# Low-rank coefficients of a batch from two matrix products instead of five

## The chip, the cores and the metric

The kernel runs on one core of one Trainium2 chip. The metric is the device time of one execution in microseconds (us), the median of three runs. The core has five engines that work side by side, each through its own instruction queue in order: TensorE (PE in the profile; its weight loads are listed apart as PEld), VectorE (DVE), ScalarE (ACT), GpSimd (POOL) and SyncE (SP), which here only issues DMA transfers.

## The reference

The input `x` has 8 batches of 3136 rows and 256 channels. The first stage is the real part of a Fourier transform over rows and channels; the second adds a low-rank mixing over the rows and a two-layer network over the channels.

```python
X = np.fft.fft(x, axis=1)
X = np.fft.fft(X, axis=2)
x = X.real
h = x.transpose(0, 2, 1) @ U @ V        # U: 3136 x 32, V: 32 x 3136
u = x + h.transpose(0, 2, 1)
out = u + np.maximum(u @ w_ch1, 0.0) @ w_ch2   # 256 -> 1024 -> 256
```

The large products run in bf16 with fp32 sums.

## The kernel before

The output is made in 49 chunks of 512 rows that run across the batch borders. The main loop has 8 slots a chunk (`first_product(c, j)`, j = 0 to 7): each slot makes one 128x512 piece of the hidden layer (two products, line 691) and ScalarE applies the relu (line 693); every second slot also makes a row tile of the chunk before (`second_product`, eight products of 128x256, line 707), which VectorE adds to the transposed input and writes to `o` (lines 713 to 716). In slot 3 `front(c + 1)` builds the input `u` of the next chunk: one product adds the low-rank part (`low_product`, line 665), VectorE adds the transform `S` or `T` (line 681).

Between these, the work of the next batch is laid into the slots by `spread`: a list of steps is spaced evenly between a first and a last slot. `fold(b)` (VectorE, lines 386 to 399, with the loads of the next batch, issued by GpSimd's queue) ends before `transform(b)`, which for batches 2 to 7 has 17 steps: eight calls of `seq`, four pairs of `even_ch` and `odd_ch`, and `lowrank`. Batches 0 and 1 are done in another way: batch 0 ahead of the loop, batch 1 with `first_channel` and `chan` in its list. A scheduler then orders the instructions of each engine; the part ahead of the loop has the order in which it is written.

`seq(b, par, typ, pn)` multiplies the folded input by tables of sines (`typ` 0) and cosines (`typ` 1) along the rows; `par` says whether even or odd rows. The tables carry 32 further columns, `NQ:QW`, that hold the matching transform of U. So each `seq` with `pn` = 1 also gives a 128x32 piece, and there are four pieces a batch: two types by two parities. Before, line 459 writes each into its own 32 columns of `TAB`, in bf16. The folded sine half has nothing in partition 0 and row 0 of the sine matrix `MSN` is zero.

The channel that the halves leave over goes its own way (`narrow`): for batches 0 and 1 in `first_channel`, for batches 2 to 7 together in `column_steps`, which loads a single channel of six batches (`cf`, `cr`). `narrow` also gives the 32 coefficients of that channel: two parities, added at line 537 to a row of `low` (batches 0 and 1) or to a 6x32 tile; `finish` then spreads the six rows over `low` with one masked product each (line 573).

`lowrank(b)` brings these together in one PSUM tile: `low` times a matrix of ones, and the four pieces of `TAB` times the channel matrices `MSN` and `MC`. Line 636 copies the first 32 rows to `TA`, which `low_product` reads for all chunks of the batch.

Of the kernel before, what the change touches and what calls it, by code (L numbers as in the profile page):

```python
# [16 lines left out]
P = 128  # L17
# [3 lines left out]
NQ = 393  # L21
# [6 lines left out]
def kernel(  # L28
# [261 lines left out]
    def kp(i):  # L290
        return KP if i == NI - 1 else PQ
# [124 lines left out]
        for par in range(2):  # L416
            yield lambda par=par: half(b, par, slice(0, 258 if b < B0 else 256))

    TAB = cpool.tile([P, 7 * R], BF16, name="tab")
    NM = NQ // 2  # L420
    HW = QW - NM

    def halves(d, g, par, typ):

        pt = psum.tile([P, 2, 256], FP32, tag="dft", name="pth", bufs=3)
        for m, tiles in enumerate(((3, 7), (1, 5))):
            for n, i in enumerate(tiles):
                nc.tensor.matmul(pt[:, m, :HW], g[:kp(i), i, P * typ:P * (typ + 1)],  # L428
                                 tabs[typ][:kp(i), i, par, NM:], start=(n == 0), stop=(n == 1))
        ev = d["ev"] = wp.tile([P, QW], FP32, tag="ev", name="ev", bufs=4)  # L430
        nc.scalar.copy(ev[:, NM:], pt[:, 1, :HW])
        back = ev[:, NM - 1:(0 if par else None):-1]
        he, ho = pt[:, 0, 1 + par:NM + 1], ev[:, NM + 1 + par:NQ]
        nc.vector.tensor_tensor(back, *((he, ho) if typ == 1 else (ho, he)), op=AL.subtract)
        nc.vector.tensor_tensor(ev[:, NM:], pt[:, 0, :HW], ev[:, NM:], op=AL.add)

    def seq(b, par, typ, pn):

        if b not in ST:
            d = ST[b] = {}  # L440
            d["A"] = wp.tile([P, HALF + 1], BF16, tag="A", name="A", bufs=1)
            d["B"] = wp.tile([P, HALF + 1], BF16, tag="B", name="B", bufs=1)
            d["S"] = wp.tile([P, HALF + 1], BF16, tag="S", name="S", bufs=2)
            d["T"] = wp.tile([P, HALF + 1], BF16, tag="T", name="T", bufs=2)
        d = ST[b]
        g = G[b % 2][par]
        if pn == 0 and (b >= B0 or b == 1 and typ == 1):
            halves(d, g, par, typ)
            return
        pt = psum.tile([P, QW], FP32, tag="dft", name="pt", bufs=3)  # L450
        for n, i in enumerate(ktiles(pn)):
            nc.tensor.matmul(pt[:], g[:kp(i), i, P * typ:P * (typ + 1)], tabs[typ][:kp(i), i, par, :],  # L452
                             start=(n == 0), stop=(n == NI // 2 - 1))
        if pn == 0:
            ev = d["ev"] = wp.tile([P, QW], FP32, tag="ev", name="ev", bufs=4)
            nc.scalar.copy(ev[:], pt[:])
            return
        ev = d["ev"]
        nc.vector.tensor_tensor(TAB[:, (2 * typ + par) * R:(2 * typ + par + 1) * R],  # L459
                                pt[:, NQ:QW], ev[:, NQ:QW], op=AL.add)  # L460
        dst = d["A"] if typ == 1 else d["B"]
        if par == 0:
            up, c0 = dst[:, HALF // 2::-2], 0
        else:
            up, c0 = dst[:, HALF // 2 - 1:0:-2], 1
        nc.vector.tensor_tensor(up, pt[:, c0:NQ], ev[:, c0:NQ], op=AL.add)

        def down():
            dn = dst[:, HALF // 2 + 2 - par:HALF + 1 - par:2]
            nc.vector.tensor_tensor(dn, *((ev[:, 1:NQ], pt[:, 1:NQ]) if typ == 1 else  # L470
                                          (pt[:, 1:NQ], ev[:, 1:NQ])), op=AL.subtract)
        if b == 0 and typ == 1:
            return down
        down()
# [4 lines left out]
    cr = cpool.tile([KP, 2, NI, NB], FP32, name="cr")  # L479
    GC = [cpool.tile([KP, NI * NB + R], BF16, name=f"gc{par}", tag=f"gc{par}") for par in range(2)]  # L480
    rows = cpool.tile([NB, S], BF16, name="rows")
    low = cpool.tile([P, (B + 3) * R], BF16, name="low")
    unit = cpool.tile([P, NB], FP32, name="unit")

    def column_zeros():
        nc.gpsimd.memset(cf[:], 0.0)
        nc.gpsimd.memset(cr[:], 0.0)
        for par in range(2):
            nc.gpsimd.memset(GC[par][:, NI * NB:], 0.0)

    def column_flips():
        nc.vector.tensor_copy(unit[:], fl[:, 1, :NB])

    def column_loads():

# [18 lines left out]
    def narrow(nb, stationary, dst, tc_, total, tag=("dft", 3), late=None):  # L514

        t = {}

        def products():
            pt = t["pt"] = psum.tile([P, QW], FP32, tag=tag[0], name="ptc", bufs=tag[1])
            for n in range(NI // 2):  # L520
                for g in range(4):
                    pn, par = divmod(g, 2)
                    i = ktiles(pn)[n]
                    nc.tensor.matmul(pt[g * R:(g + 1) * R], stationary(par, i),
                                     tabs[1][:kp(i), i, par, :],
                                     start=(n == 0), stop=(n == NI // 2 - 1))
            t["ev"] = wp.tile([P, QW], FP32, tag="ev", name="evc", bufs=4)
            nc.scalar.copy(t["ev"][2 * R:], t["pt"][:2 * R])
        yield products

        def sums(par):
            e, o = (t[k][(2 + par) * R:(2 + par) * R + nb] for k in ("ev", "pt"))
            up = dst[:, HALF // 2 - par:(0 if par else None):-2]
            dn = dst[:, HALF // 2 + 2 - par:HALF + 1 - par:2]
            nc.vector.tensor_tensor(tc_[:, par], o[:, NQ:QW], e[:, NQ:QW], op=AL.add)
            if par:
                nc.vector.tensor_tensor(total, tc_[:, 0], tc_[:, 1], op=AL.add)
            nc.vector.tensor_tensor(up, o[:, par:NQ], e[:, par:NQ], op=AL.add)
            down = lambda: nc.vector.tensor_tensor(dn, e[:, 1:NQ], o[:, 1:NQ], op=AL.subtract)
            if late is None:  # L540
                down()
            else:
                late.append(down)
        for par in range(2):
            yield lambda par=par: sums(par)

    def column_steps():
# [3 lines left out]
        def fold_c():  # L551
# [11 lines left out]
            for par in range(2):  # L563
# [1 line left out]
                                        op=AL.add if par == 0 else AL.subtract)  # L565
        yield fold_c
        yield from narrow(NB, lambda par, i: GC[par][:kp(i), i * NB:i * NB + R], rows, tc_,
                          tc_[:, 0])

        def finish():  # L570
            nc.scalar.copy(rows[:, HALF + 1:S], rows[:, HALF - 1:0:-1])
            for b in range(NB):
                nc.vector.tensor_single_scalar(low[:NB, (b + B0) * R:(b + B0 + 1) * R], tc_[:, 0],
                                               unit[:NB, b:b + 1], op=AL.mult)
        yield finish

    def first_channel(b, **kw):
        tc_ = cpool.tile([1, 2, R], FP32, name=f"tc{b}", tag=f"tc{b}")
        dst = VA[b][R:R + 1]
        yield from narrow(1, lambda par, i: G[b][par][:kp(i), i, 256:256 + R], dst, tc_,  # L580
                          low[:1, b * R:(b + 1) * R], **kw)
        mid = (HALF + S) // 2
        for lo, hi in ((HALF + 1, mid), (mid, S)):
            def turn_row(lo=lo, hi=hi):
                with tc.issue_after(LAST[0].ins):
                    nc.scalar.copy(dst[:, lo:hi], dst[:, S - lo:S - hi:-1])
            yield turn_row
# [29 lines left out]
    def across(b, ch):  # L617
# [5 lines left out]
        lo, hi = max(lo, 1), min(hi, HALF)  # L623
        nc.scalar.copy(to[:, S - hi + 1:S - lo + 1], src[:, hi - 1:lo - 1:-1])

    def lowrank(b, fill=0, tag=("dft", 3)):
        pt = psum.tile([P, 256], FP32, tag=tag[0], name="ptt", bufs=tag[1])
        for _ in range(fill):
            nc.tensor.matmul(pt[:], ones[:, :P], ones[:], start=True, stop=True)
        nc.tensor.matmul(pt[:], low[:, b * R:b * R + P], ones[:], start=True, stop=False)  # L630
        for n in range(4):
            nc.tensor.matmul(pt[:], TAB[:, n * R:n * R + P], MDT[n // 2][:],
                             start=False, stop=(n == 3))
        if b >= B0:
            nc.sync.dma_start(out=VA[b % 2][R:R + 1, :], in_=rows[b - B0:b - B0 + 1, :])
        nc.scalar.copy(TA[b % 2][:R, :], pt[:R])  # L636
# [89 lines left out]
    def transform(b):  # L726
# [4 lines left out]
                    yield lambda par=par, typ=typ, pn=pn: seq(b, par, typ, pn)  # L731
        if b < B0:
            yield from first_channel(b)
            for ch in range(4):
                for h in range(2):
                    yield lambda ch=ch, h=h: chan(b, ch * 392 + (1 if ch else 0),
                                                  (ch + 1) * 392 + 1, h)
            yield lambda: (lowrank(b), last_row(b))
            return
        for ch in range(4):  # L740
            yield lambda ch=ch: (even_ch(b, ch), across(b, ch))
            yield lambda ch=ch: odd_ch(b, ch)
# [137 lines left out]
    singles()  # L880
    ta_rows(0)
    va_zeros(0)
    nc.gpsimd.memset(TAB[:, 4 * R:].bitcast(I32), 0)
    nc.gpsimd.memset(low[:].bitcast(I32), 0)
    MDT = [MSN, MC]
    seq(0, 0, 0, 0)
    fold_pe(1, 0, 1, False)
# [17 lines left out]
    sine(MSN[:, 128:256], pd[:, 128:256], 17, 1)  # L905
    seq(0, 0, 1, 0)
    cosine(MC[:], pd[:], 17)
    nc.gpsimd.tensor_single_scalar(MC[0:1], MC[0:1], 0.5, op=AL.mult)
    for step in narrow_0[1:3]:
        step()  # L910
# [32 lines left out]
    def piece(n, h):  # L943
# [1 line left out]

    due = {0: piece(1, 0), 1: piece(1, 1), 2: piece(2, 0), 3: piece(2, 1), 8: piece(3, 0),
           9: piece(3, 1), 10: piece(0, 0), 11: piece(0, 1), 13: [lambda: last_row(0)],
           16: narrow_0[3:4], 18: narrow_0[4:5], 44: [column_flips]}

    def spread(steps, lo, hi):  # L950

# [59 lines left out]
```

## Time and profile before

| | us |
|---|---|
| median of 3 runs | 454.53 |
| lowest and highest run | 454.16, 461.81 |
| the profiled execution | 455.21 |
| its span, first to last instruction | 453.4 |
| granted TensorE clock | 0.999 |

Times in the profile count from the start of the span. `x16` is a count of instructions, `[0.53 <-PE pt L452]` an idle time of the engine just before them and what ended it. An engine's row gives start, duration, engine, line, operation, output and input tiles with their forms. Matmuls are pipelined: the duration of one reaches beyond the start of the next.

### The profile page before, as it was taken

The numbers are of one execution on the slowest core, as the hardware profiler recorded it, in microseconds if no ns is written. First come the engines' busy times: TensorE is split into PE (matmuls) and PEld (weight loads), VectorE is DVE, ScalarE is ACT, GpSimd is POOL, SyncE is SP. The second block draws the span as 40 slices with busy tenths as digits, with TensorE's granted clock in tenths as the row PEclk, the third lists the DMA queues.
The fourth block names the chain that finished last, engine by engine and source line by source line (L and its number), as shares of the span: only waits on it lengthen the run. The fifth ranks groups of instructions, "written<-read, shape, count | busy, mean of one in ns | idle before, by whom it ended". The sixth has DMA issues, their size and how long they took to land.

```text
span 453.4 us, 8081 instructions
## 1 busy us (share of the span) xinstructions
PE 441.6 (97%) x2991; PEld 321.5 (71%) x3044; DVE 347.8 (77%) x813; ACT 293.2 (65%) x563; POOL 63.4 (14%) x115
## 2 busy tenths in 40 slices
PE   8999999999999999999999999999999999999996
PEld 6556675767777777777777777777777777777774
DVE  8789999879997779877998779877898666343433
ACT  8666648657865586656765586657765586556551
POOL 8963210200112002200111002200000000000000
PEclk9999999999999999999999999999999999999999
DMA  7998999992488437662578337662343332435342
GB/s 135 214 224 148 215 146 173 182 206 71 139 207 222 94 99 211 193 181 72 149 204 215 95 116 208 194 165 72 93 117 93 88 101 74 115 90 135 83 133 95
DMA packets 103238, 65.38 MB, mean 144 GB/s; under 512 B 73794, under 2 KB 99612, under 8 KB 100452
## 3 DMA queue, kind: packets, MB, share of 16 engines
q1 hardware_dynamic: 97516, 39.10, 38.3%
q0 software_dynamic: 5664, 25.75, 21.4%
q8 instruction: 24, 0.39, 0.4%
q14 instruction: 16, 0.13, 0.1%
q10 hardware_dynamic: 18, 0.00, 0.0%
HBM read 29.33 MB, written 25.69 MB: 121 GB/s over the span
## 4 chain that ended last, share of the span: by engine, by line
PE 84%; DVE 6%; DMA 3%; issue 2%; POOL 1%; ACT 1%; SPq 1%; DVEq 0%; ACTq 0%; POOLq 0%
PE p L707 35%; PE p L691 32%; PE pt L452 5%; PE ph L665 4%; PE pth L428 2%; DMA xb<-in_x_dram,xidx 2%; DMA cr<-in_x_dram 1%; DVE eor L386 1%; PE pst L604 1%; PE pst L613 1%; SPq L508 1%; PE m L803 1%; DVE eof L386 1%; DVE u L681 1%; DVE o L716 1%
## 5 line engine op out<-in xcount | busy, mean ns | idle before, releaser
L693 ACT ACTIVATE h<-p 128x512 bf16<-128x512 f32 x392 | 223.6, 598 | 129.6 <-PE p L691 117.0
L691 PE MATMUL p<-u,w 128*128 128x512 bf16 x734 | 208.6, 379 | 2.2 <-DVE u L681 0.5
L707 PE MATMUL p<-w,h 128*128 128x256 bf16 x1568 | 204.2, 273 | 1.3
L707 PEld LDWEIGHTS <-h 128*128 128x128 bf16 x1568 | 153.0, 98 | 51.4 <-DVE o L716 0.8
L691 PEld LDWEIGHTS <-w 128*128 128x128 bf16 x784 | 105.9, 144 | 35.4 <-issue 1.7
L713 DVE TENSOR_TENSOR o<-p,ut 128x4 f32<-128x4 f32 (+1 forms) x100 | 16.4, 164 | 56.8 <-PE p L707 54.4
L55 POOL DMA_INDIRECT xf<-in_x_dram,xidx x14 | 17.8, 1271 | 184.4 <-DVE eof L386 173.0
L716 DVE TENSOR_TENSOR o<-p,ut 128x254 f32<-128x254 f32 (+1 forms) x100 | 40.9, 409 | 0.0
L715 DVE TENSOR_TENSOR o<-p,ut 128x254 f32<-128x254 f32 (+1 forms) x100 | 40.8, 408 | 0.0
L681 DVE TENSOR_TENSOR u<-ph,S 128x512 bf16<-128x512 f32 (+23 forms) x63 | 34.5, 556 | 0.0
L681 DVE TENSOR_TENSOR u<-ph,T 128x512 bf16<-128x512 f32 (+23 forms) x63 | 34.4, 557 | 0.0
L386 DVE TENSOR_TENSOR eor<-xr 99x1024 bf16<-99x1024 f32 x28 | 34.1, 1220 | 0.1
L386 DVE TENSOR_TENSOR eof<-xf 99x1024 bf16<-99x1024 f32 x28 | 33.7, 1218 | 0.0
L665 PE MATMUL ph<-va,ta 128*128 128x512 bf16 (+15 forms) x124 | 28.6, 328 | 0.1
L452 PEld LDWEIGHTS <-g 98*128 98x128 bf16 (+1 forms) x152 | 14.6, 98 | 13.0 <-issue 0.7
L459 DVE TENSOR_TENSOR tab<-pt,ev 128x32 bf16<-128x32 f32 x32 | 6.1, 191 | 17.8 <-PE pt L452 17.0
L395 DVE TENSOR_TENSOR eos<-eof,eor 99x1024 bf16<-99x1024 bf16 (+1 forms) x28 | 18.8, 687 | 0.0
L615 DVE TENSOR_TENSOR S<-evd,pst 128x392 bf16<-128x392 f32 (+1 forms) x24 | 13.6, 566 | 6.5 <-PE pst L613 6.1
L452 PE MATMUL pt<-tabs,g 98*128 98x425 bf16 x80 | 17.7, 344 | 0.0
L399 DVE TENSOR_TENSOR g<-eos 99x2048 bf16<-99x2048 bf16 (+1 forms) x14 | 17.0, 1219 | 0.0
L452 PE MATMUL pt<-tabc,g 98*128 98x425 bf16 x72 | 15.5, 344 | 0.0
L665 PEld LDWEIGHTS <-ta 128*128 128x128 bf16 (+1 forms) x128 | 11.9, 98 | 3.1 <-ACT ta L636 0.6
(190 smaller groups left out, 356.9 us busy)
## 6 DMA issues: line engine op xcount, KB each, us to landing
out_dram<-o SPq DMA_DIRECT2D x48, 512.0 KB
xr<-in_x_dram POOLq DMA_DIRECT2D x14, 784.0 KB, 6.7
xb<-in_x_dram POOLq DMA_DIRECT2D x2, 392.0 KB, 7.3
ut<-u SPq DMA_TRANSPOSE x49
w<-in_moe_w_ch_dram POOLq DMA_DIRECT2D x1, 512.0 KB, 8.5
out_dram<-o SPq DMA_DIRECT2D x4, 128.0 KB
va<-in_moe_V_dram POOLq DMA_DIRECT2D x2, 196.0 KB, 7.1
w<-in_moe_w_ch_dram POOLq DMA_DIRECT2D x1, 256.0 KB, 7.0
```

The costliest lines, as they stand in the source:

```text
L55: nc.gpsimd.indirect_dma_start(out_, None, bass.AP(t.tensor, t.offset, [[w, rows], [1, w]]), bass.IndirectOffsetOnAxis(idx, 0), element_of ...
L386: pin(nc.vector.tensor_tensor(dst[:, a, :, part * P:(part + 1) * P].rearrange("p i (k t) -> p i k t", k=2), lo, hi, op=AL.subtract if part ...
L395: pin(nc.vector.tensor_tensor(EOS[:, a, :, cols], EOF_[:, a, :, cols], EOR_[:, a, ::-1][:, :, cols], op=op))
L399: pin(nc.vector.tensor_tensor(G[b % 2][par][:, :, cols], EOS[:, 0, :, cols], EOS[:, 1, :, cols], op=AL.add if par == 0 else AL.subtract))
L452: nc.tensor.matmul(pt[:], g[:kp(i), i, P * typ:P * (typ + 1)], tabs[typ][:kp(i), i, par, :], start=(n == 0), stop=(n == NI // 2 - 1))
L665: nc.tensor.matmul(ph, TA[b % 2][:k, s * P:(s + 1) * P], VA[b % 2][:k, lo:hi], start=start, stop=True)
L681: nc.vector.tensor_tensor(u[:, s, col:col + hi - lo], ph[:, col:col + hi - lo], src, op=AL.add)
L691: nc.tensor.matmul(p1[:], W1[:, s, j::JT], k["u"][:, s, :], start=(s == 0), stop=(s == 1))
L693: LAST[0] = nc.scalar.activation(k["h"][:, j, :], p1[:], AF.Relu)
L707: nc.tensor.matmul(p2[:, t % w, :], h[:, j, rs], W2[:, j, :], start=(j == 0), stop=(j == JT - 1))
L715: nc.vector.tensor_tensor(o[:, ts, 1:P], p2[:, :w, 1:P], ut[:, ts, 1:P], op=AL.add)
L716: nc.vector.tensor_tensor(o[:, ts, P + 1:D], p2[:, :w, P + 1:D], ut[:, tT, P - 1:0:-1], op=AL.add)
```

## The change

- `TAB` holds two pieces, sine and cosine, in place of four. The four 128x32 pieces are written in fp32 to a new tile `TF`; `join_t` adds the two parities of both types in one 128x64 addition. For batch 0 VectorE does it, at the end of the last `seq`; for the other batches GpSimd, in a new step `joined(b)` of `transform(b)`, which so has one step more (18 in place of 17; 23 in place of 22 for batch 1).
- The single channel's coefficients go to partition 0 of the sine piece, and row 0 of `MSN` is set to ones by GpSimd. For batches 0 and 1 `narrow` writes its two parities to row 0 of `TF`; for batches 2 to 7 `finish` sends the six rows by one DMA to a tile `trow` on one partition, and `joined(b)` copies 32 of them on GpSimd.
- `lowrank` makes two products in place of five. `low`, `unit`, the six masked products and the additions to `low` are gone.

```diff
-    TAB = cpool.tile([P, 7 * R], BF16, name="tab")
+    TF = cpool.tile([P, 2, 2, R], FP32, name="tf")
+    TAB = cpool.tile([P, R + P], BF16, name="tab")
+    TS = TAB[:, :2 * R].rearrange("p (t r) -> p t r", t=2)
...
+    def join_t(eng):
+
+        eng.tensor_tensor(TS, TF[:, :, 0], TF[:, :, 1], op=AL.add)
...
-        nc.vector.tensor_tensor(TAB[:, (2 * typ + par) * R:(2 * typ + par + 1) * R],
-                                pt[:, NQ:QW], ev[:, NQ:QW], op=AL.add)
+        nc.vector.tensor_tensor(TF[:, typ, par], pt[:, NQ:QW], ev[:, NQ:QW], op=AL.add)
+        if b == 0 and typ == 1 and par == 1:
+            join_t(nc.vector)
...
-            if par:
+            if par and total is not None:
                 nc.vector.tensor_tensor(total, tc_[:, 0], tc_[:, 1], op=AL.add)
...
             nc.scalar.copy(rows[:, HALF + 1:S], rows[:, HALF - 1:0:-1])
-            for b in range(NB):
-                nc.vector.tensor_single_scalar(low[:NB, (b + B0) * R:(b + B0 + 1) * R], tc_[:, 0],
-                                               unit[:NB, b:b + 1], op=AL.mult)
+            nc.sync.dma_start(out=trow.rearrange("o (b r) -> o b r", b=NB), in_=tcb[:])
...
-        yield from narrow(1, lambda par, i: G[b][par][:kp(i), i, 256:256 + R], dst, tc_,
-                          low[:1, b * R:(b + 1) * R], **kw)
+        yield from narrow(1, lambda par, i: G[b][par][:kp(i), i, 256:256 + R], dst, TF[:1, 0],
+                          None, **kw)
...
+    def joined(b):
+
+        join_t(nc.gpsimd)
+        if b >= B0:
+            nc.gpsimd.tensor_copy(TS[:1, 0], trow[:, (b - B0) * R:(b - B0 + 1) * R])
...
-        nc.tensor.matmul(pt[:], low[:, b * R:b * R + P], ones[:], start=True, stop=False)
-        for n in range(4):
-            nc.tensor.matmul(pt[:], TAB[:, n * R:n * R + P], MDT[n // 2][:],
-                             start=False, stop=(n == 3))
+        for typ in range(2):
+            nc.tensor.matmul(pt[:], TAB[:, typ * R:typ * R + P], MDT[typ][:], start=(typ == 0),
+                             stop=(typ == 1))
...
             yield from first_channel(b)
+            yield lambda: joined(b)
...
             return
+        yield lambda: joined(b)
         for ch in range(4):
...
-    nc.gpsimd.memset(TAB[:, 4 * R:].bitcast(I32), 0)
-    nc.gpsimd.memset(low[:].bitcast(I32), 0)
+    nc.gpsimd.memset(TAB[:, 2 * R:].bitcast(I32), 0)
...
     cosine(MC[:], pd[:], 17)
+    nc.gpsimd.memset(MSN[0:1, :], 1.0)
...
-           16: narrow_0[3:4], 18: narrow_0[4:5], 44: [column_flips]}
+           16: narrow_0[3:4], 18: narrow_0[4:5]}
```

More of the change, by code (lines that the diff above doesn't have):

```diff
@@ L481 @@
     rows = cpool.tile([NB, S], BF16, name="rows")
-    low = cpool.tile([P, (B + 3) * R], BF16, name="low")
-    unit = cpool.tile([P, NB], FP32, name="unit")
+    tcb = cpool.tile([NB, R], BF16, name="tcb")
+    trow = cpool.tile([1, NB * R], BF16, name="trow")
     def column_zeros():
@@ L489, in column_zeros @@
             nc.gpsimd.memset(GC[par][:, NI * NB:], 0.0)
-    def column_flips():
-        nc.vector.tensor_copy(unit[:], fl[:, 1, :NB])
     def column_loads():
@@ L567, in column_steps @@
         yield from narrow(NB, lambda par, i: GC[par][:kp(i), i * NB:i * NB + R], rows, tc_,
-                          tc_[:, 0])
+                          tcb[:])
         def finish():
             nc.scalar.copy(rows[:, HALF + 1:S], rows[:, HALF - 1:0:-1])
-            for b in range(NB):
-                nc.vector.tensor_single_scalar(low[:NB, (b + B0) * R:(b + B0 + 1) * R], tc_[:, 0],
-                                               unit[:NB, b:b + 1], op=AL.mult)
+            nc.sync.dma_start(out=trow.rearrange("o (b r) -> o b r", b=NB), in_=tcb[:])
         yield finish
     def first_channel(b, **kw):
-        tc_ = cpool.tile([1, 2, R], FP32, name=f"tc{b}", tag=f"tc{b}")
         dst = VA[b][R:R + 1]
-        yield from narrow(1, lambda par, i: G[b][par][:kp(i), i, 256:256 + R], dst, tc_,
-                          low[:1, b * R:(b + 1) * R], **kw)
+        yield from narrow(1, lambda par, i: G[b][par][:kp(i), i, 256:256 + R], dst, TF[:1, 0],
+                          None, **kw)
         mid = (HALF + S) // 2
```

## The prediction

> **What bounds the kernel now.** I read the page's totals and chain first, then the busy time by stretches, then the order of time around one `lowrank`.
>
> ```profile
> span 453.4 us, 8081 instructions
> PE 441.6 (97%) x2991; PEld 321.5 (71%) x3044; DVE 347.8 (77%) x813; ACT 293.2 (65%) x563; POOL 63.4 (14%) x115
> PE 84%; DVE 6%; DMA 3%; issue 2%; POOL 1%; ACT 1%; SPq 1%; DVEq 0%; ACTq 0%; POOLq 0%
> ```
>
> TensorE is busy 97% of the span and makes up 84% of the chain that ended last. VectorE has a small part of that chain, so I looked for where. Columns of the stretches: from:to, length, busy time of each engine (instructions), clock, DMA.
>
> ```profile
> 34.00:97.40 63.40, 61.03 (x400) 42.36 (x407) 58.83 (x113) 40.46 (x80) 12.29 (x21) 1.00 0.97 171
> 97.40:390.00 292.60, 290.62 (x1989) 216.23 (x2026) 237.85 (x547) 196.30 (x380) 24.00 (x32) 1.00 0.53 141
> ```
>
> From 97.4 to 390 us TensorE lacks 2 us of being always busy, and VectorE has 292.60 - 237.85 = 54.8 us free: there a product less is time less. From 34 to 97.4 us VectorE is busy 93% of the time, and the chain, in order of time, leaves TensorE:
>
> ```profile
> 74.59 0.18 DVE low L537
> 74.78 0.60 DVE va L539
> ...
> 90.43 6.41 DMA cr<-in_x_dram
> ...
> 97.09 0.28 ACT cb L555
> ...
> PE pc L560 <- ACT cb L555: 0.8, 1, 0.8
> ```
>
> The end of that stretch is set by VectorE, then by SP's single-channel loads `cr`, then by ScalarE's copy of them; TensorE waits 0.8 us for it (last row, from the list of waits). So what batches 0 and 1 save on TensorE ahead of 97 us is only kept if that side chain moves too.
>
> **The change: three products less a batch.** The timeline of TensorE around `lowrank(1)`:
>
> ```profile
> 81.04 0.27 PE L630 MATMUL ptt<-ones,low 128*128 128x256 bf16 x1
> 81.15 0.38 PE L632 MATMUL ptt<-msn,tab 128*128 128x256 bf16 x2
> 81.36 0.38 PE L632 MATMUL ptt<-mc,tab 128*128 128x256 bf16 x2
> 81.58 1.03 PE L691 MATMUL p<-u,w 128*128 128x512 bf16 x4
> ```
>
> A product lasts 0.27 us, but the next starts 0.11 later: what counts is the step, 81.58 - 81.04 = 0.54 for five, 0.108 each. Three less are 0.324 us. For batches 2 to 7, inside the stretch that TensorE fills, that is 6 x 0.324 = 1.94 us, the main term.
>
> **Batch 0**, ahead of the loop:
>
> ```profile
> 26.86 0.69 ACT L238 ACTIVATE msn<-pd,c 128x128 bf16<-128x128 int32 x2
> 29.00 0.87 POOL L908 TENSOR_SCALAR mc<-mc 1x256 bf16<-1x256 bf16 x1 [3.71 <-ACT mc L245]
> 29.34 0.38 PE L917 MATMUL pu<-B,msn 128*128 128x512 bf16 x1
> 29.39 0.19 DVE L459 TENSOR_TENSOR tab<-pt,ev 128x32 bf16<-128x32 f32 x1
> 29.50 0.57 DVE L466 TENSOR_TENSOR A<-pt,ev 128x392 bf16<-128x392 f32 x1
> 29.77 0.27 PE L630 MATMUL ptt<-ones,low 128*128 128x256 bf16 x1
> 30.57 0.36 ACT L636 CAST ta<-ptt 32x256 bf16<-32x256 f32 x1 [1.26 <-POOL ta L227]
> ```
>
> The last piece is written at 29.58; the join then stands on VectorE between it and `A`. The trace has no 128x64 addition there. Below it stands the 0.19 of the 128x32 row, above it the 0.57 of 128x392; I take 0.2, next to the former. Both products then wait until about 29.8 instead of starting at 29.77 and end after 0.22 instead of 0.54 us: 0.3 gained less the join's delay of `A`, which the next product needs. I take 0.2. The ones for `MSN`: ScalarE has its sines done at 27.55, GpSimd stands idle 3.71 us before 29.00, and the first reader starts at 29.34. Even at the 0.87 us of the other 1x256 row it is done by 28.4 and costs nothing; beyond 29.3 it would hold TensorE one for one.
>
> **Batch 1.** TensorE's 0.32 falls ahead of the wait at 97 us. VectorE, which leads the chain there, loses the `low` addition of batch 1: 74.78 - 74.59 = 0.19. So batches 0 and 1 together keep something between 0 (the column loads do not move) and 0.2 + 0.32 + 0.8 = 1.3 us (the wait goes too); I take 0.4, next to the 0.2 of batch 0 and the 0.19 of VectorE, which is what moves the chain's head.
>
> **What VectorE and GpSimd do instead.**
>
> ```profile
> L459 DVE TENSOR_TENSOR tab<-pt,ev 128x32 bf16<-128x32 f32 x32 | 6.1, 191 | 17.8 <-PE pt L452 17.0
> L573 DVE TENSOR_SCALAR low<-tc,unit 6x32 bf16<-6x32 f32 x6 | 1.2, 219 | 0.0
> L835 POOL TENSOR_TENSOR g<-es 99x16 bf16<-99x16 bf16 x2 | 0.4, 216 | 0.1
> L936 POOL COPY me<-mc 128x128 bf16<-128x128 bf16 x1 | 0.3, 299 | 0.0
> ...
> 72.49 0.52 POOL L101 DMA_DIRECT2D xr<-in_x_dram  x1
> 73.74 0.19 DVE L535 TENSOR_TENSOR tc<-ptc,evc 1x32 f32<-1x32 f32 x1
> 82.05 1.58 POOL L55 DMA_INDIRECT xf<-in_x_dram,xidx  x1 [9.03 <-DVE eof L386]
> 107.56 0.64 SPq L635 DMA_DIRECT2D va<-rows  x1
> 115.26 0.19 DVE L459 TENSOR_TENSOR tab<-pt,ev 128x32 bf16<-128x32 f32 x1 [0.54 <-PE pt L452]
> 119.97 1.02 POOL L55 DMA_INDIRECT xf<-in_x_dram,xidx  x1 [32.75 <-DVE eof L386]
> ```
>
> The pieces stay 128x32 additions out of PSUM; in fp32 I cost them as now. The fp32 row nearest, `tc` with 0.19, gives no reason for more. The six `low` products of 0.22 (1.3 us) go, from a stretch where VectorE has time: nothing gained. GpSimd's join lies between the 0.22 of 99x16 and the 0.87 of line 908; I take 0.3, the 128x128 copy's, and 0.2 for the copy of `trow`. In the order of the built program `joined(1)` stands behind the load at 72.49 and waits for the last piece (73.74 + 0.19); it is done by 74.5 (75 at most), and `lowrank(1)` reads it at 81.04: 6 us of cover. Behind it GpSimd has the gather of 82.05, which waits for VectorE anyway. `joined(2)` waits for the piece of 115.26 and is done by 116; behind it stands the gather of 119.97. Later batches repeat this. Cover gone means one us lost for each us that the join ends after `lowrank` is due. The DMA to `trow` goes on SP's queue just before the one of 107.56; if it costs the same 0.64 to issue and as long as the 6.41 us of `cr` to land, it is there by 115 and delays neither the join nor the transposes behind it on SP by anything that is due.
>
> [...] First the rows: the same gather takes GpSimd 1.02 us at 119.97, but more where a two-input addition of VectorE runs:
>
> ```profile
> 134.90 1.22 DVE L386 TENSOR_TENSOR eor<-xr 99x1024 bf16<-99x1024 f32 x1
> 135.30 1.71 POOL L55 DMA_INDIRECT xf<-in_x_dram,xidx  x1 [9.12 <-DVE eof L386]
> ```
>
> GpSimd gave way there by 0.7 us, VectorE kept its usual 1.22. [...] By the place in the order, a join meets VectorE in the additions out of PSUM that follow each last piece, not in a fold.
>
> **What moves.** With 18 steps in place of 17, the first two pairs of `even_ch` and `odd_ch` fall one slot later. In the built order of batches 2 to 5 VectorE now has three `o` additions before, not behind, the first `S`, `T` pair, then the fold's `eor`, then `u`. In batch 3 it runs so today:
>
> ```profile
> 170.29 0.56 DVE L615 TENSOR_TENSOR S<-evd,pst 128x393 bf16<-128x393 f32 x1
> 171.24 0.16 DVE L713 TENSOR_TENSOR o<-p,ut 128x4 f32<-128x4 f32 x1
> ...
> 173.70 0.69 DVE L681 TENSOR_TENSOR u<-ph,S 128x512 bf16<-128x512 f32 x1
> 175.13 0.59 PE L691 MATMUL p<-u,w 128*128 128x512 bf16 x2
> ```
>
> The pair lasts 171.24 - 170.29 = 0.95. `o` waits for TensorE's second product, which ends about 170.9, so `o` can start 0.3 before 171.24 and the pair follows: everything behind is later by 0.95 - 0.3 = 0.65. `u` then ends at 173.70 + 0.69 + 0.65 = 175.04, and its first reader is due at 175.13. It fits by 0.1 us. I put 0 to 0.15 us of stall on each of four batches, 0 to 0.6, and take 0.2.
>
> The sum: -1.94 - 0.4 + 0.2 = -2.1 us. The profiled execution took 455.21, so 453.1 for it; it lies 0.7 above the median of 454.53, from which I forecast 454.53 - 2.1 = 452.4. With the ends of the terms (-1.94 - 1.3, and -1.94 + 0.6) it is 451.2 to 453.2.
>
> **The rivals.**
> - *Late `u`, slower.* The 0.1 us of room fails: if `u` comes later by a further pair, 0.95, TensorE stalls 0.85 in each of four batches, 3.4 us, and the result is 454.53 - 2.3 + 3.4 = 455.6. It decides from a stall of 0.6 a batch. For it: the sum of rows above leaves so little. Against: VectorE is free 54.8 us in the stretch and catches up by the next chunk.
> - *The gain stays in the waits.* The column loads come as late as before or a little later, because the `chan` steps of batch 1 and the loads of the next chunks move by a slot; one loads' issue held back 1 us, together with the 0.6 of stalls, leaves 454.53 - 1.94 + 1.6 = 454.2. For it: the wait at 97 us; against: SP's order is the same but for one DMA.
> [...]
> - *A product costs its whole 0.27 us.* Then 24 x 0.27 = 6.5 us: 448.0. The steps of 0.108 speak against it.
>
> That the change does not do what it says is out: the built order shows two products a `lowrank` and the joins where told.
>
> **How the numbers follow.** Forecast 0.66, gain in the waits 0.13, late `u` 0.12, lock 0.05, full cost 0.04. The likeliest gives 452.4. For 8 in 10 the range goes from the forecast's lower end, 451.2, over the second and the fourth case to 454.9, short of the late `u`. A difference of 2%, 9.1 us, is about what a measurement of this kernel tells from no change. The forecast is 0.5% and all priced rivals lie within 2%; a late `u` or a join held up over 2 us in most batches would pass it, 0.03, and a saving beyond all 24 products is hardly to be had, 0.01. That leaves 0.96 within.
>
> **What would show it.** In the new profile TensorE goes from one product of `lowrank` to the work behind it in 0.22 us, in all eight; the busy time between column loads and the last `lowrank` is about 1.9 us shorter. GpSimd's 128x64 additions last near 0.3 us and nothing waits for them. A wait of line 691 (its new number) for VectorE's `u`, four times, would show the late `u`; a longer wait of `pc` for `cb`, the second rival. I am wrong if the stretch behind 97 us gets no shorter, or if TensorE waits there for GpSimd.

## The result

The changed kernel takes 450.57 us in the median of six runs (449.89 to 452.13), the kernel before 454.35 in six on the same chip (453.54 to 461.81). Runs more than 1.5% above the fastest of their kernel are left out of the ratios. The ratio is 0.9917 with a 95% interval of 0.9898 to 0.9936: 3.8 us less, between 2.9 and 4.6. The forecast was 2.1 us less, with 451.2 as its lower end. The direction holds; the size is nearly twice the forecast.

The page of the changed kernel, in the lines that answer to those of before:

```profile
span 448.1 us, 8103 instructions
PE 441.1 (98%) x3020; PEld 320.1 (71%) x3020; DVE 346.2 (77%) x805; ACT 290.7 (65%) x563; POOL 66.9 (15%) x128
PE 91%; DVE 4%; ACT 3%; issue 1%; POOL 0%; DVEq 0%; ACTq 0%; POOLq 0%
```

TensorE's share of the chain rises from 84% to 91%, and the transfers (3% before) are gone from it. (The counts of matmuls cannot be compared: the first trace lacks records, 2991 for 3044 weight loads, this one has all 3020.) The five new groups of work, from the groups by line:

```profile
L465 DVE TENSOR_TENSOR tf<-pt,ev 128x32 f32<-128x32 f32 x32 | 6.1, 190 | 15.2 <-PE pt L458 13.3 <-ACT ev L462 0.2
...
L441 POOL TENSOR_TENSOR tab<-tf 128x64 bf16<-128x64 f32 x7 | 2.2, 319 | 181.8 <-DVE tf L465 180.7 <-PE p L697 1.1
L638 PE MATMUL ptt<-msn,tab 128*128 128x256 bf16 x8 | 2.2, 274 | 0.0
...
L631 POOL COPY tab<-trow 1x32 bf16<-1x32 bf16 x6 | 1.2, 200 | 0.4
...
L441 DVE TENSOR_TENSOR tab<-tf 128x64 bf16<-128x64 f32 x1 | 0.2, 225 | 0.0
```

The fp32 pieces cost 190 ns as the bf16 ones did (191), GpSimd's join 0.32 us against the 0.3 taken, its copy 0.20 as taken, VectorE's join 0.23 against 0.2. GpSimd waits 180.7 us for the pieces. The list of waits has one for a join, 0.2 us for VectorE's in batch 0, and none for GpSimd's. The two products of a `lowrank` take 0.22 us to the work behind them in batches 1 to 7 and 0.49 in batch 0, where the next product still waits.

To find the gain, both spans are cut at the first relu of chunks 0, 7, 8 and 48. Each row is a stretch: from:to, its length, busy time of PE, PEld, DVE, ACT and POOL (instructions), granted clock, DMA. The kernel before:

```profile
32.79:95.31 62.52, 61.21 (x401) 42.53 (x408) 59.38 (x115) 40.49 (x79) 13.45 (x22) 1.00 0.96 172
95.31:107.93 12.62, 11.49 (x89) 7.90 (x90) 9.67 (x29) 7.75 (x15) 0.00 (x0) 1.00 0.65 145
107.93:438.97 331.04, 328.82 (x2234) 245.54 (x2276) 248.58 (x581) 217.95 (x421) 24.00 (x32) 1.00 0.51 135
438.97:453.44 14.47, 10.03 (x77) 7.72 (x76) 4.19 (x20) 4.34 (x8) 0.00 (x0) 0.96 0.34 112
```

The changed kernel:

```profile
31.81:93.68 61.87, 60.93 (x406) 42.35 (x405) 59.00 (x113) 40.72 (x78) 13.90 (x23) 1.00 0.93 177
93.68:105.31 11.63, 11.46 (x91) 7.90 (x90) 9.55 (x28) 7.65 (x16) 0.00 (x0) 1.00 0.62 140
105.31:434.76 329.45, 329.45 (x2259) 244.76 (x2258) 247.13 (x576) 215.37 (x422) 27.18 (x44) 1.00 0.53 136
434.76:448.12 13.36, 10.08 (x78) 7.71 (x76) 4.17 (x19) 4.34 (x8) 0.00 (x0) 1.00 0.35 120
```

| stretch | before | after | difference | forecast |
|---|---|---|---|---|
| start to chunk 0 (batch 0) | 32.79 | 31.81 | -0.98 | -0.2 |
| chunk 0 to 7 (batch 1) | 62.52 | 61.87 | -0.65 | -0.2 |
| chunk 7 to 8 (column loads) | 12.62 | 11.63 | -0.99 | 0 |
| chunk 8 to 48 (batches 2 to 7) | 331.04 | 329.45 | -1.59 | -1.94 + 0.2 |
| chunk 48 to the end | 14.47 | 13.36 | -1.11 | 0 |

The fourth row, the one that I had worked out best, came nearly as forecast. The surplus stands in the others, and the last one has no edited line in it at all. The profiled pair differs by more than the medians (5.3 us against 3.8): the one execution was among the slowest of its kernel, the other the fastest. What belongs to the kernels and what to the two executions is the first question for the experiments.

### The profile page after: what moved, and what is told of

Its sections match the earlier page's. It is cut to its first block, busy times and chain, and to the rows that moved or that the text cites. A ratio compares the mean times of both kernels' runs of the same rounds, so it can differ in the third digit from the quotient of the medians.

```text
span 448.1 us, 8103 instructions
## 1 busy us (share of the span) xinstructions
PE 441.1 (98%) x3020; PEld 320.1 (71%) x3020; DVE 346.2 (77%) x805; ACT 290.7 (65%) x563; POOL 66.9 (15%) x128
## 4 chain that ended last, share of the span: by engine, by line
PE 91%; DVE 4%; ACT 3%; issue 1%; POOL 0%; DVEq 0%; ACTq 0%; POOLq 0%
PE p L713 36%; PE p L697 36%; PE pt L458 6%; PE ph L671 4%; PE pth L430 2%; DVE eor L386 1%; ACT tabs L238 1%; PE pst L605 1%; PE pst L614 1%; PE m L811 1%; DVE eof L386 1%; DVE u L687 1%; PE ptc L528 1%; ACT tabc L357 1%; PE pst L593 0%
## 5 line engine op out<-in xcount | busy, mean ns | idle before, releaser
L699 ACT ACTIVATE h<-p 128x512 bf16<-128x512 f32 x392 | 220.1, 597 | 126.7 <-PE p L697 124.3
L697 PE MATMUL p<-u,w 128*128 128x512 bf16 x784 | 213.9, 379 | 1.0 <-DVE u L687 0.5
L697 PEld LDWEIGHTS <-w 128*128 128x128 bf16 x784 | 107.0, 144 | 37.3 <-issue 1.6
L441 POOL TENSOR_TENSOR tab<-tf 128x64 bf16<-128x64 f32 x7 | 2.2, 319 | 181.8 <-DVE tf L465 180.7
L671 PE MATMUL ph<-va,ta 128*128 128x512 bf16 (+16 forms) x126 | 29.1, 328 | 0.0
L465 DVE TENSOR_TENSOR tf<-pt,ev 128x32 f32<-128x32 f32 x32 | 6.1, 190 | 15.2 <-PE pt L458 13.3
```

Of the source, the lines that this page charges most:

```text
L671: nc.tensor.matmul(ph, TA[b % 2][:k, s * P:(s + 1) * P], VA[b % 2][:k, lo:hi], start=start, stop=True)
L697: nc.tensor.matmul(p1[:], W1[:, s, j::JT], k["u"][:, s, :], start=(s == 0), stop=(s == 1))
L699: LAST[0] = nc.scalar.activation(k["h"][:, j, :], p1[:], AF.Relu)
```

## The experiments

The ratios are to the kernel before on the same chip. Three theories are told apart in the first four runs: 'products' (TensorE being earlier does all), 'order' (the additional step, which moves other steps, does the rest), 'chance' (the surplus belongs to two executions).

**A second profile of the kernel before.**

> The kernel before, unchanged, for a second profile. The changed kernel gained 3.8 us by the medians where 2.1 were forecast; by the relu's start times the surplus lies between 34 and 97 us, where ScalarE's copy of the column loads waited 0.89 us for them before and not after. Theory 'chance' (the waits of the first profile are a matter of the transfers' timing in that one execution): this second profile shows no wait of cb for cr, and chunk 8 begins about 1 us earlier relative to chunk 0 than in the first one (75.14 us there). Theory 'order' and theory 'products' (the waits belong to the kernel): a wait between 0.6 and 1.2 us again, and 75.1 us within 0.3.

Measured: 454.31 us. The waits of the column stretch and the stretch itself:

```profile
ACT cb L555 <- DMA cr<-in_x_dram: 0.7, 1, 0.7
PE pc L560 <- ACT cb L555: 0.7, 1, 0.7
```

```profile
32.62:95.15 62.53, 61.21 (x401) 42.49 (x408) 59.39 (x115) 40.47 (x79) 13.44 (x22) 1.00 0.91 174
95.15:107.61 12.46, 11.49 (x89) 7.89 (x90) 9.65 (x29) 7.74 (x16) 0.00 (x0) 1.00 0.63 139
107.61:438.63 331.02, 328.80 (x2234) 245.56 (x2276) 248.52 (x581) 217.89 (x422) 24.00 (x32) 1.00 0.52 135
438.63:452.54 13.91, 10.03 (x77) 7.73 (x76) 4.18 (x19) 4.34 (x8) 0.00 (x0) 0.95 0.35 116
```

The wait is there again, so it was no accident of one execution; its length is not fixed (0.2 us in a further profile with the same loop, two fill products less, below). The long stretches repeat to 0.02 us: differences of 0.1 there can be read from one profile. The stretch with the loads moved by 0.16 and the end by 0.56 us; there one profile is not enough.

**Three products out, nothing else.**

```diff
-        nc.tensor.matmul(pt[:], low[:, b * R:b * R + P], ones[:], start=True, stop=False)
-        for n in range(4):
+        for n in (1, 3):
             nc.tensor.matmul(pt[:], TAB[:, n * R:n * R + P], MDT[n // 2][:],
-                             start=False, stop=(n == 3))
+                             start=(n == 1), stop=(n == 3))
```

> The kernel before with two products in lowrank in place of five: the product of low and those of the two even-parity pieces are left out of the sum; all other instructions and their order are those of before. Theory 'products' (TensorE being earlier is all that matters, the waits ahead of 97 us shrink by themselves): the whole gain, -3.3 to -4.0 us, ratio 0.992. Theory 'order' (the surplus is the shifted steps'): only the forecast's terms, -1.9 to -2.3 us, ratio 0.9955, and ScalarE's wait for cr is still there, longer if anything, by 0.3 us. Theory 'chance': -1.9 to -2.6 us.

Measured: 451.27 us, ratio 0.9940 (0.9923 to 0.9958), 2.7 us less. Between the theories: chunk 0 to 7 gains 0.21, chunk 8 to 48 gains 1.98, and the wait for `cr` is gone (chunk 7 to 8 takes 11.64), where 'order' had expected it.

```profile
32.40:94.71 62.31, 61.00 (x398) 42.19 (x405) 59.32 (x115) 40.47 (x78) 13.78 (x22) 1.00 0.94 177
94.71:106.35 11.64, 11.36 (x89) 7.90 (x90) 9.68 (x29) 7.64 (x16) 0.00 (x0) 1.00 0.70 148
106.35:435.41 329.06, 326.84 (x2216) 243.91 (x2258) 248.51 (x581) 217.22 (x421) 24.01 (x32) 1.00 0.54 136
435.41:448.84 13.43, 10.04 (x77) 7.72 (x76) 4.18 (x19) 4.34 (x8) 0.00 (x0) 1.00 0.36 120
```

The main term, 6 x 0.324 = 1.94, is confirmed: 331.04 - 329.06 = 1.98. And the end is short again, 13.43, though no instruction there was touched.

**The additional step alone.**

```diff
             yield from first_channel(b)
+            yield lambda: None
...
             return
+        yield lambda: None
         for ch in range(4):
```

> The kernel before with one empty step more in transform(b), where the changed kernel has joined(b): five products, the old pieces, only the places of the steps move. Theory 'order': -1.2 to -1.8 us, ratio 0.9965, and no wait of cb for cr. Theory 'products': 0 within 0.4 us. My forecast put the moved steps at a loss of 0 to 0.6 us (ratio 1.000 to 1.0015); its rival with the late u would show here as VectorE's u ending line 691's wait four times.

Measured: 454.39 us, ratio 1.0002 (0.9993 to 1.0012). Theory 'order' fails: the moved steps are worth nothing in all. By stretches, chunk 0 to 7 gains 0.24 and chunk 8 to 48 loses 0.37 (331.41). In one point 'order' was right: the wait for `cr` is gone with five products too (chunk 7 to 8 takes 11.89). VectorE's `u` ends a wait of TensorE once, 0.5 us near 55 us, as before; the rival with the late `u` is out.

**The change without the additional step.**

```diff
+                    if b >= B0 and par == 1 and typ == 0 and pn == 1:
+                        yield lambda: (seq(b, 1, 0, 1), joined(b))
+                        continue
...
-            yield from first_channel(b)
-            yield lambda: joined(b)
+            steps = list(first_channel(b))
+            yield from steps[:-1]
+            yield lambda: (steps[-1](), joined(b))
...
-        yield lambda: joined(b)
```

> The changed kernel with joined(b) called in the step ahead of it, so that transform(b) has as many steps as before and the steps lie in the old slots. Theory 'order': -2.0 to -2.4 us, ratio 0.995, the wait of cb for cr is back. Theory 'products': -3.4 to -4.0 us, ratio 0.992, as the changed kernel. Theory 'chance': as the changed kernel, within 0.4 us.

Measured: 453.87 us in the median of twelve runs from 450.26 to 459.55, ratio 0.9969 (0.9940 to 0.9999) from ten of them. The granted clock of the execution parts the ten: five at 1.00 took 450.26 to 452.02, about as long as the changed kernel, and five at 0.992 to 0.996 took 453.44 to 456.81. The profile fell on the fastest of the latter:

```profile
ACT cb L559 <- DMA cr<-in_x_dram: 1.6, 1, 1.6
PE pc L564 <- ACT cb L559: 1.6, 1, 1.6
```

```profile
32.38:94.28 61.90, 60.83 (x398) 42.22 (x405) 58.97 (x113) 40.27 (x78) 13.88 (x23) 1.00 0.88 176
94.28:109.24 14.96, 13.12 (x89) 8.33 (x90) 9.57 (x28) 7.74 (x16) 0.00 (x0) 0.89 0.60 124
109.24:438.30 329.06, 326.85 (x2216) 243.92 (x2258) 247.73 (x576) 217.22 (x422) 27.16 (x44) 1.00 0.52 136
```

Two things follow. Chunk 0 to 7 gains 0.62 here and 0.21 with the products alone: the other 0.41 goes with VectorE's shorter work. And TensorE, earlier by these 0.62 us, ran further into the wait for the column loads, the last of which SP issued no earlier (53.35 us behind the start of chunk 0, 53.37 in the kernel before): 1.6 us instead of 0.9, and then 3.4 us at half its clock (the finer cut is below). The third stretch is as with the three products out, 329.06; in the changed kernel it is 329.45. So the additional step costs 0.38 there, with five products (0.37) and with two. The timeline of TensorE in batch 3 of the changed kernel shows where a part of it lies:

```profile
162.68 0.81 PE L697 MATMUL p<-u,w 128*128 128x512 bf16 x3
163.32 1.04 PE L713 MATMUL p<-w,h 128*128 128x256 bf16 x8
164.19 1.10 PE L697 MATMUL p<-u,w 128*128 128x512 bf16 x4
165.13 1.04 PE L713 MATMUL p<-w,h 128*128 128x256 bf16 x8
166.00 0.33 PE L605 MATMUL pst<-A,me 128*128 128x393 bf16 x1
```

Four first products in a row take 165.13 - 164.19 = 0.94 us where ScalarE still has copies ahead of the relu; elsewhere four take 0.86 or 0.87. The third of them starts at 164.70, right behind the end of a relu at 164.65. One such group stands in each of the six batches, 0.05 to 0.08 us longer than the others and 0.40 in all. The kernel with the step for batch 1 alone, below, has none of them, so this is the whole loss.

**The end of the span: a longer program again.** The end is 14.47, 13.91 and 14.40 us with five products, 13.36 to 13.43 with two. The page of the kernel before counts one block of instructions more than that of the changed kernel (24 packets with 0.39 MB in all, about 16 KB each, and 23 with 0.38):

```profile
q8 instruction: 24, 0.39, 0.4%
```

```profile
q8 instruction: 23, 0.38, 0.3%
```

The next run lengthens the changed program at the start, ahead of TensorE's waits for its input.

```diff
     busy(27)
+    pad = psum.tile([P, 512], FP32, tag="p2", name="pad", bufs=2)
+    for _ in range(24):
+        nc.tensor.matmul(pad[:1, :1], ones[:, :1], ones[:, :1], start=True, stop=True)
```

> The changed kernel with 24 products of one element behind the 27 fill products at the start, where TensorE waits for its input at 15.6 us anyway: 48 instructions more on TensorE, as many as the kernel before had. From the last matmul to the end of the span the three profiles with five products a lowrank need 4.34, 3.78 and 4.27 us and load a 24th block of 16 KB of instructions in that time; the three with two products need 3.30, 3.23 and 3.24 us and load 23. Theory 'code block' (the block that the longer program needs at the very end delays the issue of the last output writes): 24 blocks again, the last at the end, 3.8 to 4.3 us behind the last matmul, and 0.5 to 1.1 us more than the changed kernel, 451.1 to 451.7. Rival (the tail differs because of the products or by chance): 23 blocks or no delay, 3.2 to 3.3 us, 450.6 within 0.3.

Measured: 23 blocks, the end unchanged (13.37 us). The time is 451.61 us, ratio 0.9935 (0.9916 to 0.9954), and the profile shows what it lost: the wait for `cr` is back with 0.6 us (chunk 7 to 8 takes 12.33). As an experiment on the end it failed by one instruction: the padded program has 6079 instructions on TensorE, the one before 6080. It shows besides that the changed kernel too can meet the column wait.

**Two fill products less in the kernel before.**

```diff
-    busy(27)
+    busy(25)
```

> The kernel before with 25 fill products at the start in place of 27; TensorE waits for its input at 15.6 us anyway. TensorE's program gets 4 instructions shorter, 6076 in place of 6080. The padded kernel (6079) still loaded 23 blocks and ended 3.24 us behind its last matmul, so if a length decides it, it lies between 6079 and 6080. Theory 'code block': 23 blocks, 3.2 to 3.3 us behind the last matmul, and 0.5 to 1.1 us less than before, ratio 0.998, with all five products in place. Rival (the tail's delay goes with the five products in some other way): 24 blocks, 3.8 to 4.3 us, no change.

Measured: 453.89 us, ratio 0.9985 (0.9973 to 0.9996), 0.7 us less by four instructions on an engine that waits there. 23 blocks, and 13.42 us for the end. SP's issue of the last four output writes (shortest, median, longest in ns), first the kernel before, then this one:

```profile
L719 SPq DMA_DIRECT2D out_dram<-o x4: 384/404/1422, 446.9 to 450.0; - x4
```

```profile
L719 SPq DMA_DIRECT2D out_dram<-o x4: 332/339/351, 446.2 to 449.0; - x4
```

One of the four takes 1422 ns instead of 339. It is issued at 447.97 us, while the block of instructions is loaded (447.37 to 449.02). The other three profiles with such a late block show the same: the slowest issue took 870, 1046 and 1354 ns, and the end 13.91, 14.09 and 14.40 us. The DMA queues of the kernel before from 446.5 us on:

```profile
q1 hardware_dynamic: 1104, 1.05, 45.6%
q8 instruction: 1, 0.02, 1.5%
q14 instruction: 1, 0.01, 0.3%
```

**Forty padding products in the changed kernel.** The same edit as the padding above with 40 in place of 24.

> The changed kernel with 40 one-element products at the start, 6111 instructions on TensorE. Theory 'code block': 24 blocks now, the last one in the last 2 us of TensorE's work, 3.8 to 4.3 us behind the last matmul, and 0.5 to 1.1 us more than with 24 such products. Rival (two products a lowrank never have the tail's delay): 23 blocks, 3.2 to 3.3 us, and the time of the 24 within 0.4 us.

Measured: 24 blocks, but no delay (13.38 us, the four writes issued in 332 to 345 ns), 451.50 us, ratio 0.9940 (0.9918 to 0.9962). The program is 31 instructions longer than the one before, so the last block comes earlier: between 440 and 443.5 us, ahead of the four writes that begin at 443.9.

```profile
q8 instruction: 1, 0.02, 2.2%
```

So the block cost nothing in this place (13.38 us beside 13.36 in the changed kernel). Where it met the last output writes, which nothing hides, in four profiles, the end was 0.5 to 1.1 us longer. Both padded kernels are some 0.9 us slower in the median than the changed kernel was on its chip. A part of this can lie at the start, for the padding was not free: the product behind it starts at 7.16 us with 24 and at 7.91 with 40, at 6.56 in the changed kernel. Later waits for the input can take up the delay, so how much of the 0.9 us it makes, beside the wait for `cr` in the first, is not settled.

**The fold of the column three slots later**, in the kernel before, in the changed one, and in the one without the additional step.

```diff
-            spread(list(column_steps()), hi - 34, hi - 22)
+            spread(list(column_steps()), hi - 31, hi - 21)
```

> The kernel before with column_steps spread from hi - 31 to hi - 21 in place of hi - 34 to hi - 22: the fold of the single channel comes three slots later, all else as before. Theory 'side chain' (TensorE stands in line behind the column loads, 0.7 to 0.9 us at 97 us): no wait of cb for cr, chunk 0 to chunk 8 takes 74.0 to 74.4 us in place of 75.0 to 75.1, and 0.7 to 1.0 us less in all, ratio 0.998. Rival (the wait is only where a delay from earlier shows): the time stays within 0.3 us and the wait turns up elsewhere ahead of chunk 10.

> The changed kernel with column_steps from hi - 31 to hi - 21. Theory 'side chain': the changed kernel no longer waits there in its profile, so at most 0.3 us less, 450.2 to 450.7; its spread of runs gets no wider. Rival (the order of the steps itself gained the time): the same; the run is for comparison with the next.

> The changed kernel without the additional step (joined(b) called in the step ahead of it) and column_steps from hi - 31 to hi - 21. In its first form without the second edit the runs lay between 450.3 and 456.8 us: in the profile TensorE waited 1.6 us for the copy of the column loads and was then granted half its clock for 3.4 us, which chunk 7 to 8 shows as 14.95 us in place of 11.63. Theory 'side chain': with the loads out of the way no such wait, no half clock, runs within 1.5 us of each other, and 0.37 us less than the changed kernel because the steps keep their old slots: 449.8 to 450.3, ratio 0.990. Theory 'order' (the old slots cost the time by themselves): 451.5 to 452.5.

Measured: 454.68 us, ratio 1.0009 (0.9981 to 1.0037); 451.11 us, ratio 0.9934 (0.9905 to 0.9963); 450.94 us, ratio 0.9916 (0.9887 to 0.9946). The wait for `cr` is gone in all three, but the first two gain nothing: chunk 7 to 8 gets shorter because work has left it (11.03 and 11.02 us), and chunk 8 to 48 takes it back (332.22 and 330.47). In the first a wait of 0.5 us for a relu turns up between 115 and 120 us. In the second this is 0.4 us worse than the changed kernel over both stretches; the rival of the first run holds. The third was expected at 449.8 to 450.3, at least 0.6 us faster than it is, since work moved behind chunk 8 here too (330.24). But its spread is what the theory asked for: seven runs from 450.56 to 451.40, all at a clock of 0.999 or 1.00, where the same kernel with the fold in the old slots had 450.26 to 456.81 in its ten. So the spread came from the wait for the column loads. It is not the only way to a lower clock: one of the ten runs of the second kernel took 455.55 at 0.996.

**The additional step for batch 1 alone**, in the changed kernel (for the later batches `joined(b)` is called in the step ahead).

> The changed kernel with the additional step for batch 1 alone; in batches 2 to 7 joined(b) is called in the step ahead, so that their steps keep the old slots. In the empty-step run the additional step cost 0.37 us from chunk 8 to chunk 48 and gained 0.6 us up to chunk 6, where only batch 1 has run. Theory: chunk 0 to 8 as in the changed kernel (73.5 to 74.2 us), chunk 8 to 48 in 329.1 in place of 329.45 us, so 0.3 to 0.4 us less than the changed kernel: 450.2, ratio 0.991. Rival (the gain ahead of chunk 8 needs batch 2's steps moved as well): chunk 0 to 8 takes 75 us or more, with the half clock of the run without any additional step, 452 to 454 us.

Measured: 449.94 us in six runs (449.53 to 454.32), ratio 0.9912 (0.9878 to 0.9947).

```profile
32.52:94.40 61.88, 60.94 (x406) 42.39 (x405) 59.02 (x113) 40.71 (x79) 13.88 (x23) 1.00 0.91 175
94.40:106.04 11.64, 11.47 (x91) 7.91 (x90) 9.56 (x28) 7.65 (x16) 0.00 (x0) 1.00 0.75 156
106.04:435.10 329.06, 329.06 (x2259) 243.90 (x2258) 247.71 (x576) 217.22 (x421) 27.15 (x44) 1.00 0.53 136
435.10:448.46 13.36, 10.09 (x78) 7.72 (x76) 4.18 (x20) 4.34 (x8) 0.00 (x0) 1.00 0.35 120
```

As expected: 0.39 us less behind chunk 8 than the changed kernel, and nothing lost ahead of it. It beats the kernel before clearly; against the changed kernel the stretches say 0.4 us, the interval of the ratios cannot.

**The join on VectorE.** `joined(b)` calls `join_t(nc.vector)`; GpSimd keeps the copy of the row.

> The changed kernel with the join of the parts on VectorE for all batches (GpSimd only copies the single channel's row). VectorE's own join for batch 0 took 0.23 us, GpSimd's 0.32. Theory 'cover' (VectorE has 54.8 us free behind chunk 8): no change, within 0.4 us of the changed kernel, ratio 0.992. Rival (VectorE leads the chain of batch 1, and each us there is TensorE's): 0.2 us more and no more than that. [...]

Measured: 450.98 us, ratio 0.9921 (0.9896 to 0.9946). The stretches are those of the changed kernel to 0.01 us (61.88, 11.64, 329.46, 13.36). Where the addition is done makes no difference here, and GpSimd's join held up nobody.

## Why the prediction was wrong

**Right.** The price of a product by the step from one start to the next: 0.324 us a batch was measured as 1.98 / 6 = 0.33. The costs of the new operations, all within 0.03 us. The cover of GpSimd's joins: no wait for them behind batch 0, and no gain from taking them away. The chance that I called lock (0.05) stood for joins on GpSimd that hold up VectorE; no run shows such a hold-up, for with the join on VectorE the time was 450.98 us and the stretches were those of the changed kernel to 0.01 us. The full 0.27 us a product would have been 6.5 us; out. The additional step's loss, taken as 0.2 with 0 to 0.6 as bounds, was 0.38, but by another mechanism than I named: not `u` late by VectorE's new order, but first products bunched four in a row ahead of ScalarE. That it lay within the bounds was luck. Two slips had no weight: the ends of the terms give 451.3 as the lower end, not 451.2, and the 2 us that TensorE seemed to lack behind 97 us are records missing from that trace (with all records, the run with two fill products less shows 331.05 us busy in the 331.05 us of the stretch).

Batch 0 was right too, against the -0.98 of the table. From the first product of its `seq` to the first relu of chunk 0, the five profiles with all five products need 13.53 or 13.54 us and the eight with the change 13.35 to 13.37: 0.18 less, where I took 0.2. The rest of the 0.98 lies ahead of that product, in work that the change does not touch:

```profile
15.62 0.38 PE L803 MATMUL m<-xb,flip 99*99 99x512 bf16 x1 [0.30 <-DMA xb<-in_x_dram,xidx]
19.25 0.89 PE L452 MATMUL pt<-tabs,g 98*128 98x425 bf16 x4
```

```profile
18.45 0.89 PE L458 MATMUL pt<-tabs,g 98*128 98x425 bf16 x4
```

The first two rows are the kernel before, the third the changed one. In that one execution of the changed kernel TensorE had no such wait for its input; the five other profiles of changed kernels without padding start this product at 19.02 to 19.44. So 0.80 us of the profiled pair's difference belongs to the two executions.

**Wrong, first: the sum had no term for the length of TensorE's program.** I wrote where the 48 instructions were executed and not that the program is fetched during the run, in 24 loads before and 23 after. The kernel before, with 6080 instructions, is just long enough for a 24th block (6079 loaded 23), and the load falls on the last output writes; 49 instructions less, or four, and it is not fetched. Two fill products removed from the kernel before show the size without any of the change: 0.7 us (0.2 to 1.2). Without it the changed kernel would have come out near 451.3, at the edge of the range. It has nothing to do with low-rank coefficients.

**Wrong, second: "batches 0 and 1 together keep something between 0 and 1.3 us; I take 0.4".** They kept about 1.4: 0.18 for batch 0, and for batch 1 0.65 from chunk 0 to 7 and about 0.6 of the column wait. Of the 0.65, the products give 0.21. The 0.41 that came with the rest in the run without the additional step were priced at 0.19, for one `low` addition. That is the step from its start to the next start (74.59 and 74.78, in the prediction). But the addition also parts two additions to `va` that otherwise overlap. First the kernel before, then the run without the additional step:

```profile
73.97 0.59 DVE L538 TENSOR_TENSOR va<-ptc,evc 1x392 bf16<-1x392 f32 x1
```

```profile
73.49 0.59 DVE L542 TENSOR_TENSOR va<-ptc,evc 1x392 bf16<-1x392 f32 x1
73.98 0.59 DVE L543 TENSOR_TENSOR va<-evc,ptc 1x392 bf16<-1x392 f32 x1
```

From one to the other it was 74.78 - 73.97 = 0.81 us with `low` between them and is 0.49 without: 0.32, not 0.19. The copy to `unit`, which I had left out, held up the operation behind it by 0.08 (41.56 to 41.64). The stretches agree: of the 0.41, 0.08 us are gained between chunks 0 and 4 and 0.30 between chunks 4 and 5, where the `low` addition stood.

The column wait went in most profiles of kernels with two products, but not in all: chunk 7 to 8 took 12.62, 12.46 and 11.94 us in the three with five products and the old order, and 11.63, 12.33, 11.62, 11.64 and 11.64 in the five with the changed kernel's stretches. The means, 12.34 and 11.77, differ by 0.6, not by 0.99. It also went with the additional step alone and with three products out alone (one profile each), so it hangs on no single part of the change. I had taken the upper end for unlikely since TensorE's gain only lengthens that wait; without the additional step it did just that. Against it works batch 1's additional step, of which I had feared the opposite (the second rival). With the column fold in its old place, SP starts the last group of loads 50.2 to 52.8 us behind the start of chunk 0 in the six profiles with that step (52.26 in the changed kernel) and 52.9 to 53.4 in the five without; VectorE's shorter work alone left it at 53.35. How long SP needs for this group differs from profile to profile (4.6 to 7.9 us), and why is not shown, so the 0.6 is a mean and no fixed price.

The terms as measured: 0.18 for batch 0, 0.65 and 0.6 ahead of chunk 8, 1.59 behind it, 0.7 at the end, which is 3.7, beside 3.8 in the medians.

## What to carry to other kernels

When an edit removes instructions, look at the end of the span for a load of program code among the last output writes: a few instructions more or less can be worth more than the work they do (here four, 0.7 us). Price each stretch by what leads its chain, and list every small operation that leaves that engine, not the one that the edit is about. A wait just ahead of an engine that is to get faster is not a fixed loss: it grows with the gain unless the chain behind it moves too (here from 0.9 to 1.6 us), and it can be followed by a lower clock: here waits of 0.7 and 0.9 us left it at 1.00, and behind the one of 1.6 us it was 0.51 for 3.4 us. An operation that parts two others which would overlap can cost more than its own step from start to start (here 0.32 us and not 0.19).

## What the runs showed of the hardware

In the run without the additional step, TensorE's wait was followed by a stretch at half the granted clock. Its busy time in consecutive stretches, same columns as above:

```profile
92.00:95.00 3.00, 2.95 (x20) 2.13 (x20) 2.90 (x6) 1.78 (x4) 0.00 (x0) 1.00 0.84 109
95.00:97.60 2.60, 0.87 (x10) 0.63 (x8) 0.00 (x0) 1.00 (x4) 0.00 (x0) 1.00 1.23 166
97.60:101.00 3.40, 3.40 (x19) 1.47 (x20) 1.34 (x6) 1.02 (x3) 0.00 (x0) 0.51 1.06 292
101.00:104.00 3.00, 2.94 (x30) 1.89 (x24) 2.60 (x8) 1.10 (x2) 0.00 (x0) 0.99 0.05 16
```

A wait of 1.6 us cost 1.6 and then half of 3.4 us more, 3.3 in all: 14.96 us for chunk 7 to 8 against 11.63. The waits of 0.9 and 0.7 us in the kernel before cost no clock: it was 1.00 in both stretches. A finer cut puts the half clock at 97.65 to 101.06 us. Ahead of the last stretch only this one profile shows it; what length of wait it takes is not shown.

The profile counts 24 loads of instructions in queue q8 in the kernel before, 0.39 MB in all and so about 16 KB each, and 23 in the changed kernel. The number goes with the length of TensorE's program: four instructions less there made it 23 in the kernel before, and 80 more made it 24 in the changed one. With the 40 padding products the last load came ahead of the last writes and cost nothing (13.38 us for the end). In the kernel before it fell on them, with an issue on SP of 1422 ns where the kernel with two fill products less has 339 in the median, and the end took 14.47 us.
